# A fused attention and MLP kernel: batch 0's values by casting transfers, its last rows in both halves of the partitions, and w_in's descriptors held back

## The chip, the cores and the metric

The kernel runs on one core of a Trainium2 chip. Its engines are PE (TensorE, matmuls and transposes), DVE (VectorE), ACT (ScalarE), POOL (GpSimd) and SP (SyncE). Each takes its own instructions in the order in which they stand; semaphores tie the engines together. Transfers are issued from SP, ACT or POOL and share 16 DMA engines. The metric is the time of one execution in device microseconds, and the median of several runs is compared.

## What is computed

Inputs are `q`, `k` and `v` of shape (8 batches, 8 heads, 576 rows, 64), `w_in` (512 x 2048) and `w_out` (2048 x 512), all float32. The attention is a linear one with cosine weights; its result is the input of a two-layer network.

```python
theta = np.pi / 2.0 * pos / S
phi = lambda x: concat([relu(x) * cos(theta), relu(x) * sin(theta)], axis=-1)   # 64 -> 128 features
q_p, k_p = phi(q), phi(k)
kv  = einsum('bhsf,bhsd->bhfd', k_p, v)
z   = sum(k_p, axis=2)
num = einsum('bhsf,bhfd->bhsd', q_p, kv)
den = einsum('bhsf,bhf->bhs', q_p, z)[..., None] + 1e-06
x   = (num / den), heads side by side                 # 4608 x 512
out = square(relu(x @ w_in)) @ w_out                  # 4608 x 512
```

## The kernel before, in words

**Tiles.** The 576 rows of a batch are four tiles of 128 (512 rows, row 4p+j in partition p of tile j) and a tail of 64. Tails of two batches share one tile: an even batch sits in partitions 0 to 63 and an odd one in 64 to 127 (`rows`, L223). `load_main`, `load_tiles`, `load_half` and `load_tail` (L198 to L231) fetch them as float32 into fixed homes.

**Attention of one batch.** For each tile the features of keys and queries are made by ACT or DVE (`feat`, L317): relu times a column of cosines or sines, written in bfloat16. Values are cast to bfloat16 into `vext`, which holds 65 columns per head: 64 values and a one. The matmul of key features with these 65 columns (`first_kv` for batch 0, L383) gives the key-value sums and, in column 64, the sum of the key features. A copy (`first_kvz`, L399) brings the sums to SBUF. Query features are transposed on PE (L460) and copied back (L477); their matmuls with the sums (`first_num`, L407) give numerators and denominator, `first_div` (L417) divides, and the result `x` is transposed once more (`first_x_pe`, L526) and copied to `xT` (L534).

**Batch 0 is handled apart.** Its heads are split in two halves of four, so that the first half's sums (bank 4) can be finished while the second half's (bank 5) wait for data. Its tiles 0 and 1 go through `first_num` and `first_div` by halves, and tiles 2 and 3 through the ordinary `att_num` and `att_div`. The first product, `x @ w_in`, begins with pieces of 128 columns (`first_mm`, L703 to L709), as soon as parts of `xT` are there. While PE waits for data it multiplies zeros (`warm`, L347): 28 times at the start and ten times singly between other work.

**Loads at the start.** SP issues the keys of batch 0, then half of its queries. ACT issues the tails of keys and values. POOL makes the index column, then the identity, and then issues the two halves of the values (held until the cosines are computed on ACT), the other half of the queries, and w_in in four quarters along its 2048 columns (`load_w1`, L272); the transfers of w_in convert float32 to bfloat16 on their way, as all transfers from POOL into bfloat16 tiles do. Behind them POOL issues batch 1's queries, keys and values and w_out.

**The order** of all later work is written out. The kernel first records about 1,300 operations with a planner (`plan.add`), each with the engines that may run it, and then emits them in the sequence of the list `ORDER` (L20): in `17v` operation 17 goes to DVE, and `p`, `a`, `g`, `s` stand for PE, ACT, POOL and SP. The planner's durations and landing times (`plan.given`) do not reach the chip; they only document what the list was made from. Within an engine the list is the order in which work stands.

**After batch 0** the kernel overlaps batch b+1's attention with the network of batch b. From batch 2 on, products are split into seven half-size ones (`in_product`, L659, and `product`, L848); the tails of all batches form a ninth block of rows.

Of the kernel before, what the change touches and what calls it, by code (L numbers as in the profile page):

```python
# [11 lines left out]
F32 = mybir.dt.float32  # L12
# [8 lines left out]
0p 11a 17v 20v 14a 15v 18v 16a 12v 13v 22a 21v 1p 27a 26v 23p 37v 19a 28p 36v 35v 2p 3p 29a 38p 39p  # L21
42v 43a 40p 24v 44p 41a 45p 25v 46p 30v 4p 31g 56p 47a 65v 5p 48p 64a 50p 57v 6p 70a 66p 49v 7p 8p
67a 51v 9p 10p 69a 58p 74p 75p 52p 60p 68v 53a 59v 71p 61a 32g 54p 80p 72a 62p 55v 97p 81v 99p 63a
77p 98p 101p 103p 79p 100p 73v 102p 33g 105a 82p 76p 104p 84p 83v 115p 106a 85v 109p 117a 108p 107v
34g 86p 116p 87v 110p 118a 111p 112a 125p 127p 126a 88g 113a 120p 114v 121p 122a 128a 78p 134p 89g
123a 143v 129p 144a 146v 124v 147a 151p 119v 148a 136p 152v 135a 131p 90g 145v 137a 150v 130a 155p
313v 91g 132a 153p 138p 133a 156v 140p 154v 92g 180v 157p 314v 173a 141a 158p 177a 316v 159p 182a
93g 139a 179v 160p 175v 178a 94g 142v 161p 176a 149a 162p 174v 186a 184v 163p 95g 183v 185a 181v
188p 187a 189p 257s 190p 164p 191a 96g 339v 192p 260s 165p 193v 264s 166p 265s 198p 261s 167p 199v
258s 196p 194p 259s 197v 202p 168p 195v 262s 203v 200p 169p 201a 256s 206p 170p 207v 204p 171p 263s  # L30
287a 205v 293v 208p 285v 172p 209a 290v 286v 291a 216p 214v 225p 292a 269v 213a 222p 288v 226a 270v
223p 289s 266v 217p 224a 272v 234p 211v 218a 268a 232p 276v 294s 277v 267a 273v 228p 340v 279a 280v
278a 219p 428s 275v 220p 271a 274v 281p 233a 282p 221a 427s 283p 241p 227v 284a 229a 295p 230p 235a
296v 210a 306s 243p 231a 342v 305s 242a 297p 237p 426s 244a 298v 239p 238a 299s 300p 317p 240a 301v
425s 246p 245v 423s 308a 302p 248p 452a 445v 247a 251p 303v 249a 253p 450v 252a 304s 236v 307a 318p
451a 424s 367p 341v 447a 319p 309s 250v 254a 431v 320p 430a 429v 432a 453v 321p 446v 454s 448a 435v
322p 347v 348v 352p 350v 351p 349v 353a 368p 255v 323p 354a 436v 449s 369a 315v 355p 370a 356p 357a
310p 438v 371p 440v 358a 212s 311v 372p 373a 359p 580s 439a 360p 361v 374a 324p 434v 437a 465s 375p
362v 376p 581s 377v 363p 466s 388p 378v 364a 379p 215s 433v 441p 365v 579s 380a 404p 366v 389a 576s
403p 405a 442p 578s 326v 406a 443p 387p 577s 381v 325a 407p 382v 390a 408p 575s 444a 328p 409a 383v  # L40
455p 410a 329p 456v 604a 391p 412p 385v 393a 457p 607v 392p 458v 330p 394a 608a 411p 414v 459s 395p
602a 413v 460p 396p 601a 397v 573s 331p 468a 461v 312s 603a 415p 399p 467a 417v 462p 398v 332p 572s
400a 463v 416a 333p 418a 606v 464s 334p 401v 402v 335p 574s 583a 500p 469s 419v 336a 516p 337v 587a
473p 384v 609a 475p 420v 590a 610s 582v 585a 476p 386v 591a 496v 474p 477a 497v 343v 517p 605s 478a
501p 499v 518a 595v 481p 588v 502a 594v 593a 482p 592v 327s 584v 519a 498v 470p 503a 724s 520p 586a
471v 521p 522a 504p 725s 505p 589v 523a 597p 344v 338s 506a 525p 596v 720s 507a 524p 527v 721s 598p
526v 599p 723s 509p 600a 530v 508p 511v 483a 528p 611p 510v 553p 529a 612v 479p 554a 531a 537p 346v
512p 421v 613p 552p 514v 480p 614v 513a 555a 536p 538a 345v 615s 556p 744v 539a 616p 557p 742v 484a
540p 748v 722s 558a 541p 617v 747a 485p 559a 745v 486p 542a 422v 543a 618p 560p 515a 489v 544p 619v
561p 545p 546v 492p 743a 620s 562v 493p 563v 746s 547v 564p 494a 548p 532v 565a 487p 550v 549a 749v  # L50
664p 750a 566v 488p 644v 551a 751s 567v 648p 649p 645v 665p 490v 495s 650a 621p 568v 666a 491s 622p
734v 667a 878s 646v 651a 729v 875s 669p 728a 735v 668p 533v 877s 726a 652p 732v 876s 623p 731a 727v
871s 730v 654a 624p 733v 670a 872s 569v 653p 671a 570v 738p 655a 534v 673p 736a 656p 737v 625a 672p
870s 658v 657p 626a 869s 739p 535v 629p 647v 762s 674v 763s 660p 659v 740p 874s 676p 661a 571v 685p
741a 675v 684p 686a 752p 678v 630p 677a 753v 687a 627p 631a 662v 679a 906v 754p 688p 755v 628p 701p
663v 690a 756s 757p 632a 689p 702a 700p 899v 873s 691a 633p 758v 703a 472s 692p 901a 680v 693p 898a
694v 759p 704p 905a 903v 705p 889v 706a 634p 760v 707a 696p 764a 695v 761s 708p 765a 635p 904v 698v
697a 710v 709p 900a 797p 637v 699a 902s 712p 883v 640p 711v 793v 641p 891v 713a 907s 794v 798p 714v
886v 813p 799a 715v 814p 766s 636p 800a 642a 887v 801p 795v 892a 802p 882v 803a 638v 770p 890a 716v
804a 771p 1017s 717v 885a 1018s 806p 881v 884a 805p 639s 681v 815a 772p 807v 816a 773p 808v 893a  # L60
796v 767p 888v 774a 834p 879v 818p 718v 775a 817p 835a 719v 809p 880a 768v 778p 819a 1020s 779p 820a
811v 1019s 810a 822p 1021s 812a 894p 1022s 824v 821p 643s 683v 895p 1060s 896p 823v 833p 897a 1059s
850p 827v 836a 1032v 825p 769s 682v 780a 908p 838p 1031a 909v 837p 826a 776p 839a 1034v 828v 849p
840a 910p 851a 777p 911v 852a 841p 781a 854p 912s 1026a 913p 853p 1023a 914v 782p 855a 783p 1024a
1033v 1039v 1042a 843v 915p 842p 856a 916v 784p 1027a 1025a 857p 1029v 917s 858p 1040v 1028a 859v
845p 1062a 785p 786v 1041a 844v 861p 846a 1043s 789p 860v 862a 847v 1030a 945p 863v 941v 790p 864a
942v 848v 946p 1035p 1036p 791a 829v 962p 947a 944v 961p 943v 948a 1045v 918p 963a 831v 950p 964a
787v 949p 1046a 865v 965p 951a 966p 867v 920p 952a 1044v 967a 1047v 954p 866v 968a 1048s 953p 1061a
956v 1037p 969p 1038a 970p 971v 982p 792s 1049p 955v 788s 921p 830v 1063s 983a 973p 972v 957p 1050v
974a 919p 958a 922a 975v 997p 1051p 923a 998p 1052v 981p 999a 924p 984a 868v 1053s 1000a 925p 976v  # L70
985p 986p 959v 987a 1054p 960v 1002p 1001p 926p 1055v 1003a 988a 927p 977v 1004a 1056p 1006p 928a
1057v 1005p 929a 990p 989p 1008v 1058s 930p 991v 931p 1007v 992v 1009p 934v 1064p 1010a 993p 832v
937p 994a 1090v 995v 1095p 1091v 1111p 1092v 1096a 1094p 1065v 1112a 932p 1097a 1093v 1066s 933p
996a 1011v 1099p 935v 1110p 1098p 1012v 1113a 938p 1100a 1114p 1013v 1101a 1115p 1116a 1102p 939a
1103p 1104v 1117a 1069p 940s 1105v 936s 1106p 978v 1119p 1107a 1014v 1131p 1118p 980v 1132a 1130p
1120v 1070p 1133a 1121v 1122p 1071a 1124v 1147p 1108v 1123a 1134p 1015v 1148a 1067p 1125v 1136a
1135p 1146p 1109v 1137a 1068p 1149a 1139p 1126v 1072a 1150p 1189v 1151p 1152a 1138p 1190v 1075p
1153a 979v 1140v 1155p 1154p 1141v 1142p 1156v 1076p 1191v 1157v 1158p 1077a 1073p 1192v 1159a 1144v
1143a 1210p 1160v 1209p 1161v 1211a 1194p 1074p 1212a 1128v 1195a 1193p 1145v 1078a 1213p 1196a
1214p 1215a 1079p 1162v 1216a 1016v 1080p 1127v 1197p 1083v 1198p 1199a 1218p 1086p 1200a 1220v  # L80
1201p 1217p 1087p 1081p 1203v 1088a 1202p 1219v 1089s 1205p 1223v 1221p 1164v 1206a 1082p 1222a
1204v 1246p 1084v 1245p 1247a 1230p 1224v 1085s 1229p 1231a 1168p 1207v 1232a 1163v 1166p 1248a
1208v 1233p 1249p 1129v 1235a 1250p 1251a 1169p 1252v 1253a 1234p 1225v 1170a 1167p 1236a 1227v
1254p 1171a 1237p 1238p 1239v 1174p 1240v 1255p 1243v 1241p 1256v 1172p 1242a 1257v 1175p 1244a
1165v 1259v 1258p 1173p 1176a 1267p 1261a 1226v 1177a 1268p 1260v 1263v 1178p 1269a 1265v 1179p
1262v 1180p 1182v 1181p 1264v 1275p 1266v 1276p 1228v 1183v 1270p 1184s 1277a 1271p 1185p 1186p
1281p 1187a 1272a 1282p 1188s 1273g 1278p 1274g 1283a 1284a 1279p 1293p 1280a 1288p 1285v 1294a
1287g 1289p 1286g 1297p 1296g 1290v 1295g 1292s 1298a 1300a 1291s 1299s
"""


class Plan:

# [49 lines left out]
def kernel(  # L143
# [49 lines left out]

    kqv = {}
# [1098 lines left out]
    for i in range(10):  # L1295
        add("PE", 0.216, lambda: warm(1), w=[("T",)], due=20.0, after=9.2 + 0.5 * i)
# [191 lines left out]
```

## Time and profile before

| | |
|---|---|
| median of 3 runs | 272.25 us (272.23 to 272.44) |
| the profiled execution, its own time | 272.66 us |
| its span in the profile | 270.9 us |
| matmuls on PE in the span | 2,674 |
| moved by DMA | 53.38 MB |
| read from HBM | 36.70 MB |

The span runs from the first to the last instruction; the time also has what lies around it. A row of the timeline gives the start of a group of instructions on an engine, the time until its end, the line of the kernel, the operation, output and inputs, the number of instructions, and in brackets how long the engine had been idle and what ended this. `PEld` is the loading of weights into PE, which overlaps the matmuls. `POOLq`, `SPq` and `ACTq` are these engines' sequencers, which issue transfers. In the DMA views `q1` is the queue of SP, `q10` that of ACT and `q0` that of POOL. Ends of matmuls are modelled, so a PE shown as busy may contain short waits.

### The profile page before, as it was taken

How to read it: one execution, taken by the hardware profiler on the slowest of the kernel's cores; microseconds unless marked ns; L12 is line 12 of the kernel's file. 1: busy time of each engine (PE TensorE's matmuls, PEld its weight loads, DVE VectorE, ACT ScalarE, POOL GpSimd, SP SyncE). 2: the span in 40 equal slices, each digit the busy share in tenths (PEclk: the TensorE clock that was granted, in tenths of full speed). 3: DMA queues.
4: the chain of work that ended last, by engine and by line, in shares of the span. 5: the costliest groups of instructions: out<-in, count | busy, mean ns of one | idle time of the engine just before them, and what ended most of it. 6: DMA issues, size and time to landing. Idle time of an engine off the chain costs nothing.

```text
span 270.9 us, 6626 instructions
## 1 busy us (share of the span) xinstructions
PE 263.9 (97%) x2674; PEld 211.8 (78%) x2674; DVE 221.3 (82%) x458; ACT 197.1 (73%) x332; POOL 17.7 (7%) x31
## 2 busy tenths in 40 slices
PE   8899999999999999999999999999999999999993
PEld 3578556665577678998898889998988888888882
DVE  0974895878999999999999989898897999678601
ACT  2775990697778998989799999997649657375131
POOL 5555000000000000000000000000000000000013
PEclk9999999999999999999999999999999999999999
DMA  7999999999999999989999989836410300110054
GB/s 214 342 206 291 320 241 316 248 203 284 309 285 316 219 249 239 362 203 283 244 292 175 202 245 334 177 77 204 110 40 22 155 2 0 79 78 4 8 187 117
DMA packets 85342, 53.38 MB, mean 197 GB/s; under 512 B 56928, under 2 KB 81888, under 8 KB 85312
## 3 DMA queue, kind: packets, MB, share of 16 engines
q1 hardware_dynamic: 78352, 42.80, 60.6%
q0 software_dynamic: 5824, 9.83, 15.1%
q10 hardware_dynamic: 1136, 0.33, 0.5%
q8 instruction: 21, 0.34, 0.5%
q14 instruction: 9, 0.07, 0.1%
HBM read 36.70 MB, written 9.44 MB: 170 GB/s over the span
## 4 chain that ended last, share of the span: by engine, by line
PE 92%; DVE 2%; DMA 2%; POOL 1%; issue 1%; ACT 0%; POOLq 0%; DVEq 0%
PE bank L659 32%; PE bank L848 30%; PE bank L576 7%; PE bank L735 5%; PE bank L749 5%; PE abank L367 3%; PE abank L487 3%; PE bank L709 3%; DMA k<-in_k_dram 2%; PE bank L460 1%; PE bank L560 1%; DVE kp L325 1%; PE bank L392 1%; PE bank L524 0%; DVE x L425 0%
## 5 line engine op out<-in xcount | busy, mean ns | idle before, releaser
L659 PE MATMUL bank<-xT,w1sb 128*128 128x256 bf16 x336 | 48.2, 273 | 0.0
L659 PEld LDWEIGHTS <-w1sb 128*128 128x128 bf16 x448 | 42.8, 98 | 6.6
L848 PEld LDWEIGHTS <-gT 128*128 128x128 bf16 x448 | 43.7, 98 | 5.0
L675 ACT ACTIVATE gT<-bank 128x512 bf16<-128x512 f32 x56 | 32.5, 598 | 17.4 <-PE bank L659 17.0
L682 DVE TENSOR_TENSOR gT<-bank,qpTp 128x512 bf16<-128x512 f32 x56 | 36.6, 684 | 6.9 <-PE bank L659 4.8
L848 PE MATMUL bank<-w2sb,gT 128*128 128x256 bf16 x336 | 41.3, 273 | 0.0
L848 PEld LDWEIGHTS <-gs 128*128 128x128 bf16 x336 | 32.7, 98 | 3.8
L659 PEld LDWEIGHTS <-w1t 128*128 128x128 bf16 x336 | 31.7, 98 | 3.8
L1069 ACT COPY bank<-bank 128x512 f32<-128x512 f32 x56 | 31.7, 577 | 2.7 <-PE bank L659 1.7
L659 PE MATMUL bank<-qpTp,w1t 128*128 128x256 bf16 x224 | 32.9, 273 | 0.0
L592 DVE TENSOR_TENSOR gT<-gT 128x2048 bf16<-128x2048 bf16 (+1 forms) x23 | 26.9, 1173 | 1.6 <-ACT gT L585 1.0
L848 PE MATMUL bank<-w2t,gs 128*128 128x256 bf16 x224 | 28.0, 272 | 0.0
L502 DVE TENSOR_TENSOR x<-abank,rden 128x512 bf16<-128x512 f32 x30 | 20.7, 691 | 1.0
L590 ACT ACTIVATE gT<-gT 128x2048 bf16<-128x2048 bf16 x11 | 21.0, 1912 | 0.1
L1086 ACT COPY qpTp<-bank 128x512 f32<-128x512 f32 x28 | 16.1, 589 | 5.9 <-PE bank L659 4.2
L576 PE MATMUL bank<-xT,w1sb 128*128 128x512 bf16 x84 | 19.9, 379 | 0.0
L1157 DVE TENSOR_TENSOR ysb<-bank,y 128x512 f32<-128x512 f32 x14 | 9.6, 687 | 11.6 <-ACT y L1174 7.5
L782 POOL DMA_DIRECT2D out_dram<-ysb x4 | 2.4, 612 | 236.7 <-ACT ysb L1161 234.2
L659 PE MATMUL bank<-xT,w1t 128*128 128x256 bf16 x112 | 16.7, 273 | 0.0
L659 PE MATMUL bank<-zeros,w1sb 128*128 128x256 bf16 x112 | 16.2, 273 | 0.0
L749 PE MATMUL bank<-w2sb,gT 128*128 128x512 bf16 x64 | 15.4, 379 | 0.0
L735 PE MATMUL bank<-w2sb,gT 128*128 128x512 bf16 x64 | 15.3, 379 | 0.0
(122 smaller groups left out, 426.2 us busy)
## 6 DMA issues: line engine op xcount, KB each, us to landing
out_dram<-ysb SPq DMA_DIRECT2D x16, 512.0 KB, 4.2
q<-in_q_dram SPq DMA_DIRECT2D x13, 512.0 KB, 7.1
v<-in_v_dram SPq DMA_DIRECT2D x12, 512.0 KB, 5.4
k<-in_k_dram SPq DMA_DIRECT2D x12, 512.0 KB, 6.3
w1sb<-in_moe_w_in_dram POOLq DMA_DIRECT2D x4, 512.0 KB, 11.6
w2sb<-in_moe_w_out_dram POOLq DMA_DIRECT2D x4, 512.0 KB, 15.9
k<-in_k_dram SPq DMA_DIRECT2D x1, 1024.0 KB, 6.1
v<-in_v_dram POOLq DMA_DIRECT2D x2, 512.0 KB, 6.3
```

The costliest lines, as they stand in the source:

```text
L502: nc.vector.tensor_tensor(out=x[:, :], in0=n4[:, :, :, 0:D].rearrange("p b (k l) d -> p b k l d", l=2), in1=rden[:, :] .rearrange("p b (k ...
L576: nc.tensor.matmul(out=out_, lhsT=w1sb[:, kb, hb * P : (hb + 1) * P], rhs=x_block(m, kb), start=(kb == 0), stop=(kb == KB - 1),)
L590: eng.activation(out=g, in_=g, func=ACTF.Square)
L592: eng.tensor_tensor(out=g, in0=g, in1=g, op=ALU.mult)
L659: nc.tensor.matmul(out=bank[to][:, s * W : (s + 1) * W], lhsT=lhs[:, kb, (2 * u + s) * P : (2 * u + s + 1) * P], rhs=rhs[:, kb, :], start= ...
L675: nc.scalar.activation(out=g_pair(m, i, j, u), in_=bank[to][:, :].rearrange("p (s c) -> p s c", s=2), func=ACTF.Relu,)
L682: nc.vector.tensor_tensor(out=g_pair(m, i, j, u), in0=bank[to][:, :].rearrange("p (s c) -> p s c", s=2), in1=in_five(u).rearrange("p (s c) ...
L735: nc.tensor.matmul(out=bank[FIRST_Y[tt]][:, :], lhsT=gT_of(0)[:, hb, tt * P : (tt + 1) * P], rhs=w2sb[:, hb, :], start=(hb == 0), stop=(hb ...
L749: nc.tensor.matmul(out=bank[LAST_Y[s_]][:, :], lhsT=gT_of(m)[:, hb, tt * P : (tt + 1) * P], rhs=w2sb[:, hb, :], start=(hb == 0), stop=(hb ...
L848: nc.tensor.matmul(out=bank[to][:, s * DM2 : (s + 1) * DM2], lhsT=lhs[:, hb, s * P : (s + 1) * P], rhs=rhs[:, hb, :], start=(fresh and hb ...
L1069: add("ACT", psum, lambda: nc.scalar.copy(out=bank[b][:, :], in_=bank[a][:, :]), r=[("bank", a)], w=[("bank", b)])
L1086: add("ACT", psum, lambda u=u, Y=Y: nc.scalar.copy(out=in_five(u), in_=bank[Y][:, :]), r=[("bank", Y)], w=five)
```

## The change

The values of batch 0 no longer arrive as float32 to be cast by DVE and ACT: the transfers from POOL convert them and put them as bfloat16 into the first bytes of the same home. The column of ones is not beside them any more, so the sums of the key features come from matmuls of their own with a single column (`first_ones`), and the values' matmuls have 64 columns instead of 65.

The tails of batch 0's keys and values are laid in both halves of the partitions: heads 0 to 3 in partitions 0 to 63 and heads 4 to 7 in 64 to 127. The features of the tail are then 128 partitions x 256 instead of 64 x 512. The key tail is two issues on ACT, the value tail two casting issues on POOL, ahead of the identity and of the values.

The values no longer wait for the cosines. Instead the second quarter of w_in waits on POOL until the first half of the values has landed, and the rest of POOL's queue stands behind it. Six single multiplications of zeros remain of ten. The order of all planned work is a new list.

```diff
@@ loads
+    def load_first_v(half):
+        hs = slice(half * HH, (half + 1) * HH)
+        return nc.gpsimd.dma_start(
+            out=first_values()[:, hs, :, :],
+            in_=v[0, hs, 0:MAIN, :].rearrange("h (p j) d -> p h j d", j=J),
+        )
+    def load_first_key_tail():
+        kt = kqv["kt", 0] = home(inp, [P, H, D], "kt", dtype=F32)
+        for half in range(2):
+            hs = slice(half * HH, (half + 1) * HH)
+            nc.scalar.dma_start(out=kt[rows(half), 0:HH, :], in_=k[0, hs, MAIN:S, :].rearrange("h p d -> p h d"))
+    def load_first_value_tail():
+        for half in range(2):
+            hs = slice(half * HH, (half + 1) * HH)
+            nc.gpsimd.dma_start(out=first_value_tail()[rows(half), :, :], in_=v[0, hs, MAIN:S, :].rearrange("h p d -> p h d"))
...
     def load_w1(i, n):
         f0, f1 = i * DFF // n, (i + 1) * DFF // n
-        nc.gpsimd.dma_start(
+        load = nc.gpsimd.dma_start(
             out=w1sb[:, :, f0:f1],
             in_=moe_w_in[:, f0:f1].rearrange("(kb p) f -> p kb f", p=P),
         )
+        if i == 1:
+            tc.add_manual_dep(
+                load.ins, first_load["v"].ins.name,
+                mybir.DependencyInfo(mybir.DependencyClass.Sync, mybir.DependencyReason.DATA),
+                reason="most of w_in behind the first values",
+            )
@@ key-value sums of batch 0
-    def first_v(half, js, eng):
-        hs = slice(half * HH, (half + 1) * HH)
-        copy = eng.copy if eng is nc.scalar else eng.tensor_copy
-        copy(
-            out=vexts[0][0][:, js, hs, 0:D],
-            in_=kqv["v", 0][:, hs, js, :].rearrange("p h j d -> p j h d"),
-        )
+    def first_ones(half):
+        one = vexts[0][0][:, 0, 0, D:E1]
+        for j in range(NS):
+            for hh in range(HH):
+                lhsT, ps = first_keys(half, j, hh)
+                nc.tensor.matmul(
+                    out=bank[4 + half][:, hh * E1 + D : (hh + 1) * E1],
+                    lhsT=lhsT, rhs=one[ps],
+                    start=(j == 0 and hh == 0), stop=False,
+                )
...
     def first_kv(half, js):
         for j in js:
             for hh in range(HH):
+                lhsT, ps = first_keys(half, j, hh)
                 nc.tensor.matmul(
-                    out=bank[4 + half][:, hh * E1 : (hh + 1) * E1],
+                    out=bank[4 + half][:, hh * E1 : hh * E1 + D],
                     lhsT=lhsT,
-                    rhs=rhs,
-                    start=(j == 0 and hh == 0),
+                    rhs=first_values()[:, half * HH + hh, j, :] if j < J else first_value_tail()[ps, hh, :],
+                    start=False,
                     stop=(j == J and hh == HH - 1),
                 )
@@ the start
         load_main("k", 0, nc.sync)
-        load_tail("k", 0, nc.scalar)
-        load_tail("v", 0, nc.scalar)
+        load_first_key_tail()
         load_tiles("q", 0, nc.sync, slice(0, 2))
-        cosines = constants()
-        load = load_half("v", 0, nc.gpsimd, 0)
-        tc.add_manual_dep(
-            load.ins, cosines.ins.name,
-            mybir.DependencyInfo(mybir.DependencyClass.Sync, mybir.DependencyReason.DATA),
-            reason="values behind the keys",
-        )
-        load_half("v", 0, nc.gpsimd, 1)
+        constants()
+        load_first_value_tail()
+        make_identity(nc, ident)
+        first_load["v"] = load_first_v(0)
+        load_first_v(1)
         load_tiles("q", 0, nc.gpsimd, slice(2, 4))
```

In the new list DVE makes five of the eight key features of the four tiles, then the tail's sine; ACT makes the other three and the tail's cosine. DVE's next work is one sine and one cosine of the queries, a transpose copy, the copy of the first half's sums, another transpose copy, the first division, both features of query tile 2, two divisions, two copies, the fourth division. PE has the ones of the first half, the transposes of query tile 0, the first half's sums, the transposes of tile 1, a numerator, the ones and the sums of the second half, and then the other numerators.

More of the change, by code (lines that the diff above doesn't have):

```diff
@@ L263, in constants @@
         theta_scale = (math.pi / 2.0) / S
-        cosines = nc.scalar.activation(cos_col, sidx, ACTF.Sin, bias=bias_pi2[:], scale=-theta_scale)
+        nc.scalar.activation(cos_col, sidx, ACTF.Sin, bias=bias_pi2[:], scale=-theta_scale)
         nc.scalar.activation(sin_col, sidx, ACTF.Sin, bias=0.0, scale=theta_scale)
-        make_identity(nc, ident)
-        return cosines
     w1sb = wpool.tile([P, KB, DFF], BF16, name="w1sb")
```

212 lines of the change are left out of this document (109 added, 103 removed).

## The prediction

> **What bounds the kernel now.** First the page: the engines' shares and the chain that ended last.
>
> ```profile
> span 270.9 us, 6626 instructions
> PE 263.9 (97%) x2674; PEld 211.8 (78%) x2674; DVE 221.3 (82%) x458; ACT 197.1 (73%) x332; POOL 17.7 (7%) x31
> PE 92%; DVE 2%; DMA 2%; POOL 1%; issue 1%; ACT 0%; POOLq 0%; DVEq 0%
> ```
>
> The chain is 92% PE. The table by stretches tells where PE is not full (columns: busy us and instructions of each engine, granted clock, DMA share, GB/s).
>
> ```profile
> 0.00:17.70 17.70, 14.95 (x141) 8.54 (x142) 10.24 (x36) 10.61 (x20) 7.92 (x17) 1.00 0.98 261
> 17.70:34.00 16.30, 16.30 (x176) 12.03 (x173) 11.23 (x24) 11.99 (x21) 6.32 (x9) 1.00 1.16 290
> 220.00:248.00 28.00, 28.00 (x259) 25.10 (x257) 23.23 (x38) 15.59 (x27) 0.00 (x0) 1.00 0.10 39
> ```
>
> From 17.7 us PE is busy all the time. Modelled ends could hide small waits, so I check one stretch of the chain in order of time:
>
> ```profile
> 248.28 14.86 PE bank L848 x136
> ```
>
> 14.86 / 136 = 109 ns each, against 0.87 us for eight elsewhere on that chain: no waits. So the product's work is a fixed block, and the time moves with the moment at which it begins. The opening is read in the timeline (start, length, engine, line, operation).
>
> ```profile
> 0.84 0.40 POOL L254 IOTA sidx<- 128x4 f32 x3 [0.39 <-POOLq L1472]
> 4.13 1.67 POOL L218 DMA_DIRECT2D v<-in_v_dram  x2 [2.26 <-ACT sin_col L265]
> 5.79 0.89 POOL L210 DMA_DIRECT2D q<-in_q_dram  x1
> 6.67 3.56 POOL L274 DMA_DIRECT2D w1sb<-in_moe_w_in_dram  x4
> 6.97 0.72 DVE L325 TENSOR_SCALAR kp<-k,cos_col 128x512 bf16<-128x512 f32 x1 [5.47 <-DMA k<-in_k_dram]
> 8.00 0.62 DVE L325 TENSOR_SCALAR kp<-k,cos_col 128x512 bf16<-128x512 f32 x1
> 9.85 0.99 DVE L325 TENSOR_SCALAR qp<-q,cos_col 128x512 bf16<-128x512 f32 x2
> 10.29 0.70 ACT L321 ACTIVATE kpt<-kt,cos_col 64x512 bf16<-64x512 f32 x1
> 10.60 1.05 PE L460 MATMUL bank<-ident,qp 128*128 128x128 bf16 x16 [1.30 <-DVE qp L325]
> 11.11 1.08 DVE L378 CAST vext<-v 128x512 bf16<-128x512 f32 x3
> 11.92 0.67 PE L392 MATMUL bank<-vext,kp 128*128 128x65 bf16 x16
> 12.17 0.62 ACT L378 CAST vext<-v 128x512 bf16<-128x512 f32 x1
> 12.86 0.38 ACT L403 CAST kvz<-bank 128x260 bf16<-128x260 f32 x1
> 13.71 0.38 ACT L403 CAST kvz<-bank 128x260 bf16<-128x260 f32 x1 [0.47 <-PE bank L392]
> 14.16 0.16 DVE L422 TENSOR_SCALAR den<-bank 128x4 f32<-128x4 f32 x1 [0.58 <-PE bank L410]
> 14.91 0.15 DVE L422 TENSOR_SCALAR den<-bank 128x4 f32<-128x4 f32 x1
> 17.12 0.42 DVE L425 TENSOR_TENSOR x<-bank,rden 128x256 bf16<-128x256 f32 x1
> 17.77 1.73 PE L709 MATMUL bank<-xT,w1sb 128*128 128x128 bf16 x28
> 19.55 0.39 PE L709 MATMUL bank<-xT,w1sb 128*128 128x128 bf16 x4
> 19.78 0.41 PE L487 MATMUL abank<-kvz,qpTp 128*128 128x65 bf16 x8
> ```
>
> Keys land, features, value casts, key-value sums, divisions, and at 17.77 the first product. The reader is to see that four divisions run one behind the other, 0.75 us apart (14.16 to 14.91), and that the fourth, which ends at 17.54, holds the product up. The landings come from the issue rows (size, then us from issue to landing):
>
> ```profile
> k<-in_k_dram SPq DMA_DIRECT2D x1, 1024.0 KB, 6.1
> q<-in_q_dram SPq DMA_DIRECT2D x1, 512.0 KB, 7.8
> v<-in_v_dram POOLq DMA_DIRECT2D x2, 512.0 KB, 6.3
> w1sb<-in_moe_w_in_dram POOLq DMA_DIRECT2D x1, 512.0 KB, 8.8
> ```
>
> The keys were issued at 0.74 and the queries at 1.27, so they are there at 6.9 and 9.1; the values at 10.3 and 11.4 (4.13 and 4.97, plus about 6.3); the first quarter of w_in at 15.5 (6.67 + 8.8). That last one leaves 2.2 us before 17.77: the product may come forward by that much.
>
> **The change part by part.** I lay the new order of each engine out by hand with these durations.
>
> *POOL's queue.* New in front are two value-tail issues; the nearest row is the key tail of batch 1 (the second of these):
>
> ```profile
> 16.92 0.90 POOL L202 DMA_DIRECT2D q<-in_q_dram  x1 [6.69 <-ACT xT L534]
> ...
> 19.44 0.73 POOL L228 DMA_DIRECT2D kt<-in_k_dram  x1
> ```
>
> At no more than 0.73 each they end by 2.7; the identity moves behind them (about 0.6 with its gaps), and the first value issue stands at about 3.3 instead of 4.13, as it no longer waits for the cosines. Two values (1.67), the queries' second half (0.89) and w_in's first quarter (0.89) end at 6.75, before the first key feature (6.97). The second quarter then waits for the first values (about 10.4); behind it stand the third and fourth, batch 1's queries and everything else on POOL. Three issues of 0.89 end at 13.1. What hides this is the first quarter, still in flight to 15.5; without that cover the gap would be up to 3 us of DMA. Batch 1's queries went out only at 16.92 before, so nothing behind is late, and its values, which now also wait until PE has read the first ones, stand behind those. Zero.
>
> *Key features.* The two 128x512 features that met POOL's w_in issues took 0.72 and 0.62; a pair without (9.85, two in 0.99) shows 0.47 each, some 0.40 apart when pipelined. With w_in's issues gone I take 0.40 for DVE's five key features: 6.97 to 9.05. The tails in both halves of the partitions are 256 wide instead of 512: 0.25 on DVE and 0.4 on ACT instead of 0.47 and 0.70. Both engines are through the keys at 9.3; before, ACT ended the last one at 10.99.
>
> *Casts.* Four value casts and the tail's (DVE 1.08 + 0.41, ACT 0.62) go. DMA bears the conversion. w_in's transfers convert already, and no row has a price per piece of the values' size, so from both sides: with the bytes read they take as long as now (0); priced per piece like w_in's (below) a half takes 2.5 instead of 1.3 us. I take +0.1 a half, as reading bounds both: landings 10.4 and 11.8.
>
> *Ones.* 40 new matmuls of one column, 20 a half. The nearest rows are the 65-column ones, which load the same 128x128 weights: 16 of them in 0.67 (38 ns apart, less the last one's tail), and 40 in batch 1's sums:
>
> ```profile
> 39.98 1.32 PE abank L367 x40
> ```
>
> That is 33 ns; the 128-column product, 28 in 1.73, gives 56 as the upper end. I take 36, nearest to the short ones: 0.72 a half. The first 20 run from 9.25 (end of the warm-up) to 10.1, while PE waited for query features anyway. The second 20 stand in line ahead of the second half's values: that costs the path 0.72.
>
> *The line after it.* Query transposes 10.1 to 10.6; first key-value sum 10.6 to 11.5 (values needed at 10.6, there at 10.4); copy to 11.9; first numerator 12.0; first division 12.4 to 13.2, where before it began at 14.16. Second ones 12.2 to 12.9, second sum 12.9 to 13.8, copy to 14.3, so 0.2 later than before (14.09). But DVE has now one division behind it and both features of the third query tile too (13.2 to 14.1), and works at the other three from 14.0: ends 14.85, 15.6, 17.15. PE reaches the first product at 16.1, above w_in's 15.5.
>
> *PE from there.* Before the second numerator group (19.78 in the old trace) PE still has 32 product matmuls of 128 columns, 16 transposes and the third tile's numerators to do: 48 at about 56 ns (the 28 products above, less the tail) are 2.7, the numerators (the row at 19.78, less its tail) 0.3. From 16.0, where the last two of these transposes before the product begin, it gets there at 19.0: 19.78 - 19.0 = 0.78 gained.
>
> *The value tails* share the rounds of the DMA engines with the keys' last packets. Without any overlap that costs 0; with all 512 pieces ahead of the keys' end 0.57. Rows for such a piece, in the microsecond 6 to 7 (packets, MB, share of 16 engines):
>
> ```profile
> q1 hardware_dynamic: 430, 0.23, 74.1%
> q10 hardware_dynamic: 371, 0.09, 41.4%
> ```
>
> A 256 B piece takes 0.414 x 16 / 371 = 18 ns, 512 of them 0.57 us of all engines. The tails did that before in another queue; I take 0.1. The Trainium skill, "DMA: Bandwidth & Descriptors", section Specifications, speaks against this part: transfers under 512 B are read, modified and written. These rows show 28 ns for 512 B and 18 for 256 B, no doubling; if converting to 128 B doubled the piece, the tails would cost another 0.57 and the gain would shrink to about 0.2.
>
> *The rest of the order* is new as well. PE cannot gain where it is full; a late neighbour could cost 0.4 at most here and there. I take 0. The end stays as it is.
>
> Sum against the profiled execution: span 270.9 - 0.78 + 0.1 = 270.2; around it lie 272.66 - 270.9 = 1.76; so 272.0. The median of the runs is 0.41 below the profiled one: 271.6.
>
> **The rivals.**
>
> *Values overtake the queries (slower).* The wait on the cosines kept the values' pieces out of the queries' way. Rows of a stretch where both flow, 8.0 to 8.3:
>
> ```profile
> q0 software_dynamic: 23, 0.09, 78.1%
> q1 hardware_dynamic: 57, 0.03, 30.9%
> ```
>
> There the queries get 190 pieces a microsecond, against 430 without values at 6 to 7. If the values start to flow 0.8 earlier, 0.8 x 430 = 344 query pieces fall into this rate: 1.8 us for what took 0.8. The queries land at about 10.1 to 10.5, and as their features come right behind the keys', nearly all of it is paid: from 9.9 on the gain is gone, at 10.4 the loss is 0.45, with the keys 0.3 late too 0.75. Time 272.8. For it: the earlier issue. Against it: the tails come first on that queue and leave the other one. The Trainium skill, same page, section Queues, rings and completion order, says that an engine takes turns between queue rows packet by packet; by that rule this rival holds, and the rows above agree that both flow at once.
>
> *Weights or values late (slower).* If converting costs per piece as in w_in's own transfers, both halves take 2.4 longer and w_in's first quarter lands at 17.9:
>
> ```profile
> q0 software_dynamic: 203, 0.21, 124.3%
> ```
>
> (13 to 14 us; 203 pieces of 1 KB written.) The product then begins at 18.1: 273.4 with what is paid behind. Against it: these pieces read twice the bytes of a value's.
>
> *Hidden anyway (no change).* One-column matmuls at 60 ns, or keys 0.4 to 0.7 late, eat the gain: PE gets to the second numerators at 19.4 to 19.8, 272.0 to 272.3.
>
> **How the numbers follow.** Forecast 0.48; overtaking 0.22; late transfers 0.08; hidden 0.22, of which most lies inside 0.2% (0.54 us, about what can be told from no change). Faster by more: 0.48 and a little of the last, 0.50; within: 0.20; slower: 0.30. The likeliest's own range is 271.2 to 272.0 (no key delay, ones at 33 ns and 0.25 for the hand layout; keys 0.3 late and 0.2 for the layout). To leave out no more than 2 in 10 it reaches over the overtaking case, and as far again below the likeliest's own end: 270.9 to 273.1.
>
> **What would show it.** Right: the first product at about 16.1, key features of 0.47 on DVE, a first division near 12.4, second numerators near 19.0, PE full after that. Wrong: queries landing past 9.9, keys past 7.3, w_in's first quarter past 16.5, ones more than 40 ns apart, or PE waiting after 20 us, above all between 30 and 55 us, where batch 1 lands no earlier than before.

## The result, and the profile after

| | before | changed |
|---|---|---|
| median of the runs beside each other | 272.32 us | 275.24 us (274.47 to 275.94, four runs: two near 274.6, two near 275.9) |
| ratio | | 1.0106, 95% interval 1.0072 to 1.0141 |
| profiled execution, its span | 272.66, 270.9 us | 274.47, 272.7 us |

The forecast was 271.6 us and faster; the changed kernel is slower by 1.1%. The page of the changed kernel shows PE as full as before, and a chain in which transfers have 4% instead of 2%; the full chain line of the page puts 3% on the key tail at the start and 1% on a store at the end:

```profile
span 272.7 us, 6703 instructions
PE 264.5 (97%) x2702; PEld 213.1 (78%) x2710; DVE 217.8 (80%) x452; ACT 199.2 (73%) x333; POOL 18.5 (7%) x33
q8 instruction: 21, 0.34, 0.5%
PE 91%; DMA 4%; ACT 2%; POOL 1%; issue 1%; ACTq 0%; DVE 0%; POOLq 0%
```

The timeline of the changed kernel, cut to four places (opening, 26 to 29 us, 138 to 140 us, end):

```profile
8.76 0.51 ACT L354 ACTIVATE kpt<-kt,cos_col 128x256 bf16<-128x256 f32 x1 [0.75 <-DMA kt<-in_k_dram]
12.60 0.54 PE L414 MATMUL bank<-vext,kp 128*128 128x1 bf16 x16
12.87 0.16 DVE L461 TENSOR_SCALAR den<-bank 128x4 f32<-128x4 f32 x1
16.30 0.61 PE L748 MATMUL bank<-xT,w1sb 128*128 128x128 bf16 x8
19.12 0.41 PE L526 MATMUL abank<-kvz,qpTp 128*128 128x65 bf16 x8
...
26.64 1.03 PE L615 MATMUL bank<-xT,w1sb 128*128 128x512 bf16 x4
26.75 0.49 DVE L358 TENSOR_SCALAR qp<-q,cos_col 128x512 bf16<-128x512 f32 x1 [1.11 <-DMA q<-in_q_dram]
27.69 1.22 PE L499 MATMUL bank<-ident,qp 128*128 128x128 bf16 x16
...
137.97 0.72 ACT L354 ACTIVATE qp<-q,cos_col 128x512 bf16<-128x512 f32 x1 [0.66 <-DMA q<-in_q_dram]
138.57 1.03 PE L887 MATMUL bank<-w2sb,gT 128*128 128x256 bf16 x8
139.07 1.07 ACT L1108 COPY bank<-bank 128x512 f32<-128x512 f32 x2
139.71 0.60 PE L698 MATMUL bank<-xT,w1sb 128*128 128x256 bf16 x4
...
141.70 1.22 PE L698 MATMUL bank<-xT,w1sb 128*128 128x256 bf16 x8
...
264.94 0.37 ACT L832 COPY ysb<-bank 128x256 f32<-128x256 f32 x1 [2.74 <-DMA out_dram<-ysb]
265.21 0.59 ACT L1213 COPY y<-bank 128x512 f32<-128x512 f32 x1
265.78 1.04 PE L887 MATMUL bank<-w2sb,gs 128*128 128x256 bf16 x8
266.85 0.69 DVE L1196 TENSOR_TENSOR ysb<-bank,y 128x512 f32<-128x512 f32 x1 [0.33 <-PE bank L887]
267.57 1.34 SPq L821 DMA_DIRECT2D out_dram<-ysb  x2
269.01 0.58 SPq L829 DMA_DIRECT2D out_dram<-ysb  x1
```

- **Opening: as forecast.** First product at 16.30 (forecast 16.1), second numerators at 19.12 (19.0; before 19.78): 0.66 gained.
- **28 us: 0.36 lost.** Four 512-column matmuls take 4 x 0.216 = 0.86, so the transposes of batch 1's queries could begin at 27.50; they begin at 27.69. Sixteen take 1.22, where sixteen took 1.05 at 10.60 before. They wait for features that wait for batch 1's queries, which landed at 26.7 (25.8 before) and which the new order wants earlier: before, PE began with these queries at 28.98.
- **139 to 142 us: 0.46 lost.** Eight matmuls of 0.109 end at 139.44, the next begins at 139.71 (0.27), behind a copy of ACT (L1108) that stands behind a feature that waited for queries. The eight at 141.70 take 1.22 instead of 1.03 (0.19).
- **End: 1.61 lost.** PE's last eight end at 266.82, and the span 5.9 later.

The same end in the timeline of the kernel before:

```profile
265.59 1.04 PE L848 MATMUL bank<-w2t,gT 128*128 128x256 bf16 x8
265.79 0.69 DVE L1157 TENSOR_TENSOR ysb<-bank,y 128x512 f32<-128x512 f32 x1 [1.31 <-PE bank L848]
266.51 1.35 SPq L782 DMA_DIRECT2D out_dram<-ysb  x2
266.66 0.37 ACT L793 COPY ysb<-bank 128x256 f32<-128x256 f32 x1 [2.20 <-PE bank L848]
267.95 0.58 SPq L790 DMA_DIRECT2D out_dram<-ysb  x1
```

There PE ends at 266.63 and the span 4.3 later. Behind PE's last eight stand one short copy of ACT and small stores; in the new order DVE's last sum (1.06 later than before) stands there, with all of SP's stores behind it. In sum: -0.66 + 0.36 + 0.46 + 1.61 = 1.77, and the spans differ by 1.8. This is the account of one execution near 274.6; the medians differ by 2.9, and what makes the two runs near 275.9 longer isn't in it.

### The profile page after: what moved, and what is told of

Its sections match the earlier page's. It is cut to its first block, busy times and chain, and to the rows that moved or that the text cites. A ratio compares the mean times of both kernels' runs of the same rounds, so it can differ in the third digit from the quotient of the medians.

```text
span 272.7 us, 6703 instructions
## 1 busy us (share of the span) xinstructions
PE 264.5 (97%) x2702; PEld 213.1 (78%) x2710; DVE 217.8 (80%) x452; ACT 199.2 (73%) x333; POOL 18.5 (7%) x33
## 3 DMA queue, kind: packets, MB, share of 16 engines
q0 software_dynamic: 7136, 9.37, 15.8%
## 4 chain that ended last, share of the span: by engine, by line
PE 91%; DMA 4%; ACT 2%; POOL 1%; issue 1%; ACTq 0%; DVE 0%; POOLq 0%
PE bank L698 32%; PE bank L887 29%; PE bank L615 7%; PE bank L788 5%; PE bank L774 5%; PE abank L400 3%; PE abank L526 3%; DMA kt<-in_k_dram 3%; PE bank L748 3%; PE bank L499 2%; PE bank L599 1%; DMA out_dram<-ysb 1%; PE bank L431 1%; PE bank L563 0%; POOL out_dram L821 0%
## 5 line engine op out<-in xcount | busy, mean ns | idle before, releaser
L698 PE MATMUL bank<-xT,w1sb 128*128 128x256 bf16 x336 | 47.5, 273 | 0.1
L714 ACT ACTIVATE gT<-bank 128x512 bf16<-128x512 f32 x56 | 32.6, 597 | 13.9 <-PE bank L698 13.6
L698 PEld LDWEIGHTS <-w1t 128*128 128x128 bf16 x336 | 32.3, 98 | 4.0
L1108 ACT COPY bank<-bank 128x512 f32<-128x512 f32 x56 | 31.4, 582 | 1.9 <-PE bank L698 1.2
L698 PE MATMUL bank<-qpTp,w1t 128*128 128x256 bf16 x224 | 32.0, 273 | 0.0
L631 DVE TENSOR_TENSOR gT<-gT 128x2048 bf16<-128x2048 bf16 (+1 forms) x21 | 24.8, 1190 | 0.0
L629 ACT ACTIVATE gT<-gT 128x2048 bf16<-128x2048 bf16 (+1 forms) x13 | 23.9, 1844 | 0.3 <-DVE gT L738 0.2
L624 ACT ACTIVATE gT<-bank 128x512 bf16<-128x512 f32 x24 | 13.9, 599 | 3.5 <-PE bank L615 3.5
L774 PE MATMUL bank<-w2sb,gT 128*128 128x512 bf16 x61 | 14.8, 379 | 0.3 <-issue 0.2
```

Source lines behind the costliest of these rows:

```text
L624: nc.scalar.activation(out=gT_of(m)[:, hb, :], in_=bank[to][:, :], func=ACTF.Relu)
L629: eng.activation(out=g, in_=g, func=ACTF.Square)
L631: eng.tensor_tensor(out=g, in0=g, in1=g, op=ALU.mult)
L698: nc.tensor.matmul(out=bank[to][:, s * W : (s + 1) * W], lhsT=lhs[:, kb, (2 * u + s) * P : (2 * u + s + 1) * P], rhs=rhs[:, kb, :], start= ...
L714: nc.scalar.activation(out=g_pair(m, i, j, u), in_=bank[to][:, :].rearrange("p (s c) -> p s c", s=2), func=ACTF.Relu,)
L774: nc.tensor.matmul(out=bank[FIRST_Y[tt]][:, :], lhsT=gT_of(0)[:, hb, tt * P : (tt + 1) * P], rhs=w2sb[:, hb, :], start=(hb == 0), stop=(hb ...
```

## Experiments

### Which stretch of the new order loses it

Four mixes of the two lists. Up to 27.1 us of PE the lists contain nearly the same work.

```diff
-ORDER = the new list
+e1: new list to PE's 27 us, then the old one      e2: kernel before, new list from the same point
+e3: new list to 201 us, then the old one          e4: new to 27 us, old to 201 us, new again
```

> The changed kernel with its new order only up to PE's 27.1 us; from there the work stands in the order of the kernel before. Theory (the opening gains 0.6 us and the later part of the new list loses it and more): no waits at 28, at 140 and after the last product, so 272.3 - 0.6 = 271.7 us (271.4 to 272.1), with PE's second numerators near 19.1 and no transfer among the last waits. Rival (converting transfers and the wait of w_in's descriptors make data late throughout, whatever the order): still at least 274, with batch 1's queries, keys or values ended last before waits on PE.

> The kernel before, transfers, casts and opening untouched, with the work behind PE's 32 us in the new order. Theory: it has the loss without the gain: 272.3 + 1.65 (end) + 0.45 (the waits at 140) + 0 to 0.35 (those at 28, as batch 1's queries land 0.9 earlier here) = 274.4 to 274.8 us, with the wait of a copy for the store of its home at the end. Rival (late data by the new transfers): 272.2 to 272.6.

> The changed kernel with the order before from 201 us on (PE's clock of the profile). Theory: the wait of a copy for the store of the previous use of its home at the end goes, 1.65 us: 272.8 to 273.4 us with some of the other waits left. If the end is only where a loss of earlier shows: 274.4 or more.

> New order up to 27 us, the order before from there to 201 us, the new order again from there. Theory: the opening's gain and the end's loss alone: 271.7 + 1.65 = 273.3 us (273.0 to 273.7). Rival (the middle, 27 to 201 us, makes the end late): 271.7.

| | median, us | ratio to before (95%) |
|---|---|---|
| e1 | 273.31 (272.36 to 274.48) | 1.0024 (1.0009 to 1.0040) |
| e2 | 277.63 (276.11 to 279.01) | 1.0178 (1.0148 to 1.0209) |
| e3 | 273.00 (272.37 to 273.76) | 1.0009 (0.9997 to 1.0020) |
| e4 | 275.32 (274.36 to 275.51) | 1.0081 (1.0063 to 1.0100) |

e2 lost more than was expected, in waits of 0.7 at 97 us and 1.4 at 103 us behind DMA transposes and at its end; e4 too, with a wait of 0.95 at 150 us. (Waits of PE are counted here from where its next matmul could have begun; the brackets of the rows count from the modelled end of the last one and show 0.16 less.) Still, e3 and e4 settle the end: with the old one the changed kernel's 1.0106 falls to 1.0009, and the new one puts 0.0057 (1.5 us) back on e1. But e1 is a miss: 271.7 was expected. The opening's gain is there in its profile (numerators at 19.06), and yet the runs are slower than before and spread over 2 us. Something in the old, unchanged part costs. PE has one visible wait there, of 0.4 us at 150 us, for DVE's work on the last tile of `x` that a DMA transpose brings. The profile is of one of e1's fastest runs (272.46), so what the others lost is not seen.

### PE ahead, or its code elsewhere

Two theories for e1. A: a lead of PE (its being ahead of its old times) is lost, since transfers don't come earlier. B: the lead is good, but the 40 ones (less four zeros) put all later PE instructions 72 places further in the code. A 16 KB transfer of code (`q8 instruction`) runs after some 255 PE instructions on average (21 of them for the 2,674 matmuls and 2,674 weight loads recorded), so each falls on other work than before.

```diff
 e5 (before), four matmuls of the first product at 24 us; leaves out part of the product
-                rhs=x_block(m, kb)                  # 512 columns
+                rhs=x_block(m, kb)[:, 0:1, 0:P]     # 128 columns
 e6 (before) and e7, e9 (e1): the 28 opening multiplications of zeros, by their columns (FP is 512)
-        [FP] * 28
+        e6: [FP] * 19 + [100] * 45     e7: [FP] * 5 + [96] * 115     e9: [FP] * 12 + [64] * 108
```

> The kernel before, order and transfers untouched, with four 512-column matmuls of the first product at 24 us narrowed to 128 columns (they leave out part of the product), so that PE runs 4 x 0.16 = 0.64 us ahead from 25 us on, with each instruction at its place in the code. Theory A (a lead of PE is lost in the middle, where work waits for transfers that do not come earlier): 272.4 to 273.3 us against 272.66 of before, with waits of PE on DVE work behind DMA transposes between 90 and 175 us. Theory B (the lead is good, what costs is that PE's instructions stand elsewhere in the code, so that the 16 KB transfers that bring the code meet other DMA transposes): 272.66 - 0.64 = 272.0.

> The kernel before with the nine last of its 28 opening multiplications of zeros cut into 45 of 100 columns: the same time for PE, but all later PE instructions stand 72 further in the code, as in the changed kernel. Theory A: as before, 272.4 to 272.9. Theory B: as slow and as spread as the first experiment, 273.0 to 273.9, with the code's 16 KB transfers some 3 us earlier relative to the work and the waits at other places.

> The first experiment (new opening, old order from 27 us) with its opening multiplications of zeros cut into 120, which moves all later PE instructions by 184 more, 256 in all against the kernel before: 256 instructions are one 16 KB transfer of code, so the transfers fall on the same work as before. Theory B: the opening's gain shows, 271.8 to 272.2 us. Theory A: as the first experiment, 272.9 to 273.6.

| | lead | code moved by | median, us | ratio (95%) |
|---|---|---|---|---|
| e5 | 0.64 | 0 | 272.00 (271.80 to 272.55) | 0.9976 (0.9966 to 0.9987) |
| e6 | 0 | 72 | 273.77 (272.85 to 274.09) | 1.0030 (1.0012 to 1.0047) |
| e7 | varies | 256 | 272.69 (272.18 to 275.14) | 1.0005 (0.9983 to 1.0027) |

A falls for this lead, which begins at 25 us and comes out to the last tenth. B holds for the kernel before: with the code moved and no other work, the kernel before loses about 0.3%, and its profile shows where. First e6, then the kernel before, the same place in the timelines; DVE makes L642 (L641) from the transposed tile and PE needs that:

```profile
143.87 1.19 SPq L520 DMA_TRANSPOSE xT<-xt  x1
...
151.07 0.43 DVE L642 TENSOR_TENSOR qpTp<-xT 128x512 bf16<-128x512 bf16 x1 [1.63 <-DMA xT<-x]
151.55 0.60 PE L660 MATMUL bank<-qpTp,w1t 128*128 128x256 bf16 x4 [1.18 <-DVE qpTp L642]
```

```profile
142.13 2.25 SPq L519 DMA_TRANSPOSE xT<-xt  x1
145.78 1.23 SPq L519 DMA_TRANSPOSE xT<-x  x1
149.15 0.41 DVE L641 TENSOR_TENSOR qpTp<-xT 128x512 bf16<-128x512 bf16 x1
150.22 0.60 PE L659 MATMUL bank<-qpTp,w1t 128*128 128x256 bf16 x4
```

And the DMA view of 145.5 to 148.7 us (packets, MB, share of 16 engines; then us from issue to landing), e6 first, before second:

```profile
q1 hardware_dynamic: 1540, 0.74, 160.6%
q8 instruction: 1, 0.02, 2.2%
issues: line engine op xcount, KB each, median us to landing
xT<-x SPq DMA_TRANSPOSE x1, 5.2
```

```profile
q1 hardware_dynamic: 1764, 0.55, 96.8%
...
xT<-x SPq DMA_TRANSPOSE x1, 2.9
```

The transpose is issued at 145.76 and 145.78 and lands 5.2 and 2.9 us later: the slack at PE (149.15 + 0.41 to 150.22, 0.66) is gone and 1.3 us more. A code transfer lies in its flight in e6 and none does before. Over all 19 profiles of this study (these two kernels and 17 experiments) this transpose took 3.7 to 5.2 us (mean 4.56) in the 12 with a code transfer in its flight, 2.8 to 3.9 (mean 3.27) in the 7 without. But in e6 the lateness is older than the code transfer in this flight, which begins at 148.04. The transpose ahead on SP's queue was issued 1.74 later (143.87 instead of 142.13) and landed at 150.13 instead of 147.88; this one lands 0.8 behind it in both. Loads that SP issued between 133 and 137 us already flew up to 1.3 us longer, with an earlier code transfer, of 136.7, in flight. So what delays the queue is argued from coincidences and stays open; that the code's place costs is shown by e6.

e7 has the code in place (256 = one transfer) and no wait at 150, but its small multiplications ended at 8.6 us, PE idled, and the granted clock was 0.67 in the stretch from 10 to 12 us. So it was made again with PE kept busy:

> As the experiment with lead and code in place (new opening to 27 us, old order behind it, 256 PE instructions more in all ahead of the ones), but the 92 extra multiplications of zeros are made from the last 16 of the 28, 108 of 64 columns, so that PE stays busy until 9.5 us and its clock stays at 1.0 from 6 us on. Theory B (code position): 271.8 to 272.2 us, second numerators near 19.1, no wait of PE behind a DMA transpose at 150. If the 272.69 before was not the opening but the lead itself lost in the middle: 272.6 again.

e9: 272.60 (272.23 to 275.47), ratio 1.0011 (0.9991 to 1.0031), no wait at 150, numerators at 19.37. The gain of 0.4 in its profile is the opening's, but B expected more: a miss, as e7 was. The 256 instructions brought a code transfer of their own into the opening (at 11.7 us; the first of e1 is at 15.8), and the queries' second half (issued at 4.88) lands 9.1 us after its issue instead of 8.3 in e1. The intervals of e7 and e9 overlap that of e1, so these runs don't show that the place of the code is what e1 lost.

### The end

```diff
 e10 (changed kernel): block 8's second half in the home of the keys
-                ys[m, i] = home(mlp, [P, 2, DM], "ysb", i, F32)
+                ys[m, i] = home(inp, [P, H, J, D], "k", dtype=F32), as [P, 2, DM], where (m, i) == (B, 1)
 e11 (changed kernel): zeros as in e9, code 256 places from before
```

> The changed kernel, order untouched, with a home of its own for the second half of the last block's result, so that ACT's copy no longer waits for the store of batch 7. If that wait, which stands on the chain, makes the end late: 1.0 to 1.6 us less than the changed kernel's 275.2, so 273.6 to 274.2. If it is the new order of the last products (ACT's copy of product 5, at 265.21, waits for PE anyway; DVE's two last sums stand 1.0 apart behind it, the second one behind PE's very last product): 0 to 0.3 less, 274.9 to 275.2, with the end of the page unchanged but for the copy.

> The changed kernel, order untouched, with 92 more multiplications of zeros in the opening as in the experiment beside it, so that PE's code stands 256 instructions behind that of the kernel before instead of 72. Theory B, if the new list's own middle is sound at that place: the waits at 139 to 142 us (0.45) and the upper cluster of its runs (275.9) go, 274.0 to 274.4 us; the end's 1.65 and the 0.35 at 28 stay. If code position has no part in it: 274.5 to 275.9 in two clusters as before.

e10: 274.89 (274.16 to 275.76), ratio 1.0085 (1.0067 to 1.0104). SP's last issue moves from 269.01 to 268.87. The wait for the store, though on the changed kernel's chain, is hardly what sets the end in that profile; the order of the last products is. (The profile of e10 is of its fastest run.)

e11: 276.46 (276.43 to 276.53), ratio 1.0138, a miss. Its waits at 28 and 140 are gone (with numerators only at 19.56), but the end is later still, in the timeline and the DMA view of e11:

```profile
266.57 0.37 ACT L833 COPY ysb<-bank 128x256 f32<-128x256 f32 x1 [4.71 <-PE bank L888]
...
270.22 0.56 SPq L830 DMA_DIRECT2D out_dram<-ysb  x1
```

```profile
q8 instruction: 1, 0.02, 0.9%
...
out_dram<-ysb SPq DMA_DIRECT2D x1, 512.0 KB, 4.6
```

Here batch 7's last store, issued at 261.89, lands 4.6 us later instead of 2.6, with a code transfer at 264.4 in its flight (the row names PE, but the copy's own product was long done); it took 5.0 in e2 too, with one at 265.1. Then the wait in ACT's queue does decide: the copy starts at 266.57 instead of 264.94. The new order made the end depend on a landing on which the old one did not. This would explain the changed kernel's second cluster at 275.9, but e10, without that wait, still has runs from 274.2 to 275.8: the cluster stays open.

### The held descriptors and the key tail

```diff
 e8 (e1)
-        if i == 1: tc.add_manual_dep(load.ins, first_load["v"].ins.name, ...)
 e12 (e9), e13 (e1)
-            nc.scalar.dma_start(out=kt[rows(half), 0:HH, :], ...)
+            (nc.scalar, nc.sync)[half].dma_start(out=kt[rows(half), 0:HH, :], ...)
```

> The first experiment without the wait of w_in's second quarter for the first values; POOL issues all of w_in from 5.8 us on, beside DVE's key features. Either theory of the later part: the opening loses what the wait gave, key features 0.2 to 0.4 us later on DVE and the values 0.3 to 1.0 later behind w_in, second numerators at 19.4 to 20.0 instead of 19.1; batch 1's queries land at 25.8 instead of 26.7. 273.2 to 274 us; if the late landing of batch 1's loads is what costs, less than the first experiment, 272.6 or so.

> As the experiment with lead and code in place and the clock kept, but the second half of the key tail is issued by SP right behind the keys instead of by ACT behind the first half. In the profiles so far that half landed at 8.5 to 9.3 us where the whole tail landed at 7.0 to 7.1 before, and the second numerators came at 19.06 to 19.74. Theory (this landing is what makes the opening's gain small and unsteady): it lands near 7.2, DVE and ACT do not wait for it, second numerators at 18.8 to 19.1, time 271.6 to 272.1 us with a narrower spread. Rival (the spread is of the middle): 272.6 as without it.

> The same edit of the key tail, without the 92 extra multiplications of zeros, so that PE's code stands 72 instructions behind that of the kernel before, as in the changed kernel. Theory B (code position): the same opening, but the wait of PE at 150 us behind a late DMA transpose comes back, 0.4 to 1.3 us: 272.4 to 273.2. If the place of the code is of no account: 271.6 to 272.1 as its neighbour.

e8: 273.31, ratio 1.0022 (1.0010 to 1.0035), as e1. Holding back w_in does give DVE its 0.4 us key features (the five end at 8.8 us; without the hold at 9.8), but numerators stand at 19.12 without it and at 19.06 with it (e1): DVE was not what the opening waited for.

ACT was, and behind it the key tail. Its second half, issued by ACT at 1.48, landed at 8.4 to 9.3 us in all profiles with it there, and with the latest landings (9.30 in e3, 9.05 in e4) came the late numerators (19.74, 19.49). Timeline of e13, where SP issues it behind the keys:

```profile
7.91 0.49 ACT L354 ACTIVATE kpt<-kt,cos_col 128x256 bf16<-128x256 f32 x1
...
18.30 0.41 PE L526 MATMUL abank<-kvz,qpTp 128*128 128x65 bf16 x8
...
39.10 1.06 PE L400 MATMUL abank<-vext,kp 128*128 128x65 bf16 x30 [0.55 <-DVE vext L376]
```

In e13 it lands 5.5 us after its issue at 1.26, ACT doesn't wait, and the opening gains 1.48. Of that 0.71 go at 39.1, where PE waits for batch 1's values, which land at 38.2 (37.9 before). e13: 273.19 (272.05 to 273.83), ratio 1.0010 (0.9992 to 1.0027), five of its runs below 272.6 and six near 273.6 (the profile is of one of the first). e12, with the code in place: 272.41 (272.11 to 272.87), ratio 0.9992 (0.9980 to 1.0004), narrow, and the best version found; it is no different from before, and a miss (271.6 to 272.1 was expected). Its tail landed at 6.97, yet its numerators came only at 19.53: the code transfer at 11.7 is in its opening too, and its queries' second half lands at 14.1 (12.8 in e13).

### Two misses and one half

```diff
 e14 (e13), e15 (e1): zeros in float32
-        28 times lhsT=zeros[:, 0:P], rhs=zeros[:, :]
+        14 times lhsT=wide[:, 0:P], rhs=wide          # wide = zeros[:, :].bitcast(F32), 256 columns
 e16 (e13), e17 (e6): eight second-layer matmuls ahead of those that wait at 150 us
-... 633p 634p 791p 806p 807p 629p ...
+... 633p 634p 629p 791p 806p 807p ...
```

> The key tail's second half behind the keys on SP, old order from 27 us on, and the 28 opening multiplications of zeros replaced by 14 in float32 (256 columns, each as long as two), so that later PE instructions stand only 30 further in the code than in the kernel before and no extra transfer of code falls in the opening. Theory B: second numerators near 18.3 as without the code change, no wait at 150, at most the wait at 39 us for batch 1's values (0.7): 271.3 to 272.0 us, the first version below the kernel before. If the lead is lost in the middle in any case: 272.4 or more.

> The same with the key tail as in the changed kernel (both halves from ACT): the changed kernel's opening and the old order from 27 us, code moved by 30 instead of 72. Theory B: the first experiment's 273.3 without the wait at 150, and second numerators at 19.1 to 19.7: 271.9 to 272.6 us. If code position is of no account: 273.3.

> The key tail behind the keys (second numerators at 18.3), old order from 27 us, code 72 further as in the changed kernel, and one operation moved on PE: eight matmuls of a second-layer product whose inputs are long there (0.87 us) go ahead of the three groups that wait at 150 us for the last transposed tile. Theory B: of the waits of 0.4 to 1.3 us at 150 that the shifted code brought, 0.87 is covered: slow runs (273.5 without the move) become 272.6 to 272.9, median 272.1 to 272.5. If the loss of the shifted code is spread over many places: 273.2 as without the move.

> The kernel before with its PE code moved by 72 instructions (273.77 in the experiment on this alone, with one wait of 1.35 at 151.5 us) and the same operation of PE moved ahead of that wait. Theory B: the wait shrinks by 0.87: 272.7 to 273.1 us. If the wait at 150 is only where a general lateness shows: 273.6 to 273.9, with the wait elsewhere.

e14 gave 272.91 (1.0015, 0.9997 to 1.0033) and e15 273.92 (1.0049, 1.0031 to 1.0066). The code was not shorter: the trace has 28 multiplications of zeros for the 14 written, and code transfers begin at 15.8 and 16.1 us as in e1 (15.8). So they repeat e13 and e1, with waits of 0.8 and 1.3 at 150 us.

e17: 273.25, just above the 272.7 to 273.1 expected, ratio 1.0017 (1.0006 to 1.0028) against 1.0030, with overlapping intervals: the wait at 150 is covered, but a new one of 0.57 stands two groups later, behind a copy of ACT that the moved work no longer covers:

```profile
152.17 0.60 PE L660 MATMUL bank<-qpTp,w1t 128*128 128x256 bf16 x4
153.17 0.60 PE L660 MATMUL bank<-xT,w1sb 128*128 128x256 bf16 x4 [0.40 <-ACT bank L1070]
```

e16 is a miss and did no better than e13: 273.25, ratio 1.0015 (1.0004 to 1.0025), with waits of 0.39 at 151, 0.57 at 153 and 0.31 at 159.

In the eight profiles with the old order at 150 us and the code 72 places on (e1, e3, e4, e6, e8, e13, e14, e15), that transpose took 4.1 to 5.2 us and PE waited 0.4 to 1.3 us in all but one (e13, whose lead was already spent); in the five with the code in place (before, e5, e7, e9, e12) it took 2.9 to 3.9 and PE never waited.

## Why the prediction was wrong

**The step that failed** is "The rest of the order is new as well": it gave that part at most 0.4 "here and there", took 0, and said "The end stays as it is". The profile shows 0.82 in the middle and 1.61 at the end, and e3 and e4 put 1.5 to 2.6 us on the end (in ratios 0.0057 and 0.0097). The new list was compared on the engines only up to the second numerators; its last 15 us, where nothing hides anything, were not laid out. There the order of the last products is different, DVE's last sum follows PE's last product, and an ACT copy waits for a store; that wait is the small part (e10, without it: 1.0085 against 1.0106, with overlapping intervals). The 0.82 of the middle is the profile's alone: e3, which keeps the new middle, is no slower than e1, which doesn't (1.0009 and 1.0024).

**A term was missing altogether:** the place of PE's code. "PE cannot gain where it is full" counted the 40 ones by their time (0.72 a half) and not as 72 instructions by which every later code transfer shifts. e6 prices that alone at 0.3% (0.8 us; 1.1 by medians). None of the rivals held it. That it costs in the changed kernel itself is not shown: its profile has no wait at 150 us, the account of 1.8 us closes without it, and with the code in place (e11) it was slower. Why the opening's gain does not show in e1 therefore stays open in part.

**Right, in the profiled run:** the first product (16.30 for 16.1), second numerators (19.12 for 19.0), the first division within 0.5 (12.87 for 12.4), and POOL's hold "Zero" (e8: no difference). But "nothing behind is late" was not so: batch 1's queries landed at 26.73 (25.78 before), with the hold or without it (26.72 in e8). The 20 ones of the second half took 0.65 (12.60 to 13.25) for the 0.72 taken; within the 16 of the row they start 25 ns apart ((0.54 - 0.16) / 15, where 0.16 is the modelled length of one; the 65-column row from which 38 was read gives 32 in the same way, with 0.19). A lead at this place is worth its length: e5. One reading of rows was loose: the pair of features at 9.85, taken as free of w_in's issues, begins while these run (6.67 to 10.23); that the issues slow the features is seen in e8.

**Right in part by luck:** the size of the opening's gain, 0.66 for 0.78 (0.68 with the tails' 0.1), in which two errors met. "Both engines are through the keys at 9.3" took the key tail to be there by then; its second half landed at 8.67, ACT idled 0.75 for it and was through at 9.88. The estimate of 0.1 for the tails sharing the rounds priced pieces and not what an issue second in its queue waits for. Without that wait the opening gives 1.48 (e13), against 0.78 forecast, so what stands around it was priced too long by about 0.7; some 0.3 of that is the keys, which landed at 6.6 and not at 6.9.

**The rivals.** Overtaken queries: not seen, they landed at 9.1 as before. Late weights: not seen, w_in's first quarter landed at 15.6, as forecast. Keys late: in part, through the tail; in e3 the numerators at 19.74 are no gain at all. "PE waiting after 20 us", the last of the signs named, is what came, though at 28, 139 and the end.

## What to carry to other kernels

When a list or a schedule is made anew, lay out its last stretch first: every late step there is paid in full, and a wait for a transfer there can grow by 2 us. When instructions are added to a full engine, count them also as code: move them alone (same time, other number) and see what the kernel before does, before anything is said of the change itself. A gain at the opening is only as steady as the landing behind which it stands; look at it in several profiles.

## What the runs showed of the hardware

- Code arrives through the same DMA engines as data: `q8` moved 0.34 MB in 21 packets, 16 KB each, and their 0.5% of 16 engines' span (0.005 x 16 x 272.7 / 21) is 1.0 us of one engine each. Over the 608 DMA transposes of the 19 profiles, those with such a transfer in flight took 5.34 us on the mean (209), the others 3.89 (399); a long flight is also likelier to meet one, and the single transpose above was late before it met one, so neither shows by itself that the code transfer delays the other. Nearest to it are the 225 stores issued after 255 us, where little else moves: eight took more than 3.6 us, each with a code transfer in its flight, but 17 others that met one took 2.3 to 2.7. The Trainium skill, "Runtime: NRT & Kernel Launch", section Terms, says that an engine's instruction memory is refilled in 16 KiB blocks; the packets agree.
- The same transfer may take very different times: the DMA transposes of `x` landed between 2.7 and 7.7 us after their issue (228 of them in the 19 profiles); a part of this is the transfer ahead on the same queue.
- A second 64 KB issue on ACT's queue landed 6.9 to 7.8 us after its issue (10 profiles), the same issue behind 1 MB on SP's queue 5.5 to 5.7 (four).
